# A skipping first turn of TensorE's loop, fold 6 behind values 7, and aligned starts with hinted ends on the other engines

## The chip, the cores and the metric

The kernel runs on one core of a Trainium2 chip. Time is device microseconds (us) of that core. Three runs of the kernel before gave a median of 185.13 us (184.97 to 185.88). The profiled execution took 185.13 us; from its first to its last instruction the profile counts a span of 183.2 us, and the other 1.93 us lie around it.

A core has five engines with an instruction stream each: TensorE (PE in the profile; PEld is its weight load), VectorE (DVE), ScalarE (ACT), GpSimd (POOL) and SyncE (SP). They wait for each other by semaphores. Loads and stores run on 16 DMA engines. Instructions come to an engine by DMA too; the profile lists those transfers as queues of kind "instruction".

## The reference

One decoding step of attention over a sliding window, with grouped heads: 32 sequences, 32 query heads, 8 key/value heads of 128 columns, and the last 512 of 2048 cached positions.

```python
W = min(4096, max(256, Sk // 4))                      # 512
q = (x @ wq).reshape(B, Sq, Hq, Dh).transpose(0, 2, 1, 3)
k = repeat(k_cache[:, :, Sk - W:, :], 4, axis=1)
v = repeat(v_cache[:, :, Sk - W:, :], 4, axis=1)
scores = einsum("bhqd,bhkd->bhqk", q, k) * (Dh ** -0.5)
o = einsum("bhqk,bhkd->bhqd", softmax(scores), v)
out = o.transpose(0, 2, 1, 3).reshape(B, Sq, Hq * Dh) @ wo
```

All inputs are bfloat16: `x` is 32x1x512, the caches are 32x8x2048x128, `wq` is 512x4096 and `wo` 4096x512. The windows of keys and values are 33.5 MB each, `wq` and `wo` 4.2 MB each: 75.5 MB have to be read.

## The kernel before, in words

The 32 sequences are worked in eight groups of four (q = 0 to 7, called quarters below, as each fills the 128 partitions with four sequences). For each of them 4 MB of keys and 4 MB of values are loaded, with one partition per sequence, head and block of 128 positions (32 KB in a row). There are two key buffers (`K_sb`) and two value buffers (`V_sb`); `wq` first lies in the second value buffer, and `wo` at the end in the first key buffer.

SyncE issues all loads but `x`, in the order of `LOADS` (L34): after `wq`, keys 0 and 1, values 0, keys 2 and 3, values 1, and from there keys and values in turn, each as soon as its buffer is free. Keys q wait for VectorE's second turn of keys q-2, values q for TensorE's values q-2. Values 5 to 7 come in halves, and `wo` in three pieces (`WOP`, L40, rows 0 to 16, 16 to 28 and 28 to 32), which wait for the keys of quarter 6 to be turned. `x` is issued by ScalarE (L199 to L202), ahead of everything else on that engine.

The work on a quarter has these steps; the letters are those of the order strings at the top of the file, a digit is the quarter:

- T: VectorE transposes the keys in two halves (L511, 4.4 us each).
- S: TensorE's scores, two halves of 16 matmuls (L340). GpSimd spreads the queries for them (L309).
- M, X, N: VectorE's row maximum, ScalarE's exponential with its sum, VectorE's division.
- E: TensorE brings the probabilities to the rows of the values (L356), and ScalarE copies them out (G, L574).
- B: VectorE and ScalarE each spread four heads of them into a block diagonal (L530, L578).
- P: TensorE's values, 128 matmuls over 32 groups (L367), in parts such as `P0.0.16`.
- C: VectorE or ScalarE copy the four row blocks out of PSUM (L536, L584). The last quarter is copied in halves, I (L541, L589).
- F: TensorE's fold, four float32 matmuls with a 0/1 matrix (L379), and D: ScalarE's copy of it into `o_sel` (L592).

TensorE runs a head (`PE_HEAD`, L20: scores of quarters 0 and 1, E0 and E1), then a loop (L430) of four turns with two rounds each, written by `PE_ROUND` (L21), then a tail (`PE_TAIL`: fold 7) and the output projection (L449), 128 small matmuls with four column groups side by side. Inside the loop the groups of S and E are skipped in the last turn by a branch (L443), as there are no quarters 8 and 9. Values of semaphores to wait for are computed from the loop's counter into registers (`looped`, L433). VectorE and ScalarE run their lists `DVE_OPS` and `ACT_OPS` (L24, L29) without a loop, and end with two copies each of the output; SyncE then stores it. The fold writes to a PSUM bank given by `f_bank` (L182): bank 2 of the half of PSUM that the quarter's values use, and bank 2 for fold 7.

The scores, sums, folds and copies are put in order by hand in these strings; a helper (`needs`, L105) turns them into waits. `Waits` (L218) leaves out waits that an engine has already made.

Of the kernel before, what the change touches and what calls it, by code (L numbers as in the profile page):

```python
# [21 lines left out]
PE_TAIL = "F7"  # L22
# [8 lines left out]
G5 C3.0.4 B5.4.8 D3 X6 G6 C4.0.4 B6.4.8 D4 X7 G7 C5.0.2 B7.4.8 D5 C6.0.2 D6 I7.0.0 I7.1.0 I7.0.1 I7.1.1 D7  # L31
# [15 lines left out]
def bass_standalone__sliding_block_cached__sampling_kernel(  # L47
# [25 lines left out]
    real = lambda w: w[0] not in "SE" or int(w[1:].split(".")[0]) < NQ  # L73
# [54 lines left out]
    with ExitStack() as es:  # L128
# [53 lines left out]
        def f_bank(q):  # L182
            return ps[:, 2] if q == NQ - 1 else ps[:, 4 * (q % 2) + 2]
# [14 lines left out]

        for b0, b1 in X_PARTS:  # L199
            nc.scalar.dma_start(  # L200
                x_sb[b0:b1, :], x[b0:b1].rearrange("b s d -> b (s d)")
            ).then_inc(sem_x, 16)  # L202
# [11 lines left out]
        def rows(cache, q, r0=0, r1=R):  # L214
            return cache[4 * q:4 * q + 4, :, SK - W:, :].rearrange(
                "b h (k r) d -> (b h) k (r d)", k=KB)[:, :, r0 * DH:r1 * DH]

# [98 lines left out]
        def _(pe):  # L316
# [132 lines left out]
            for j, (i0, i1) in enumerate(WOP):  # L449
                pe.wait_ge(sem_wo[j], 16)  # L450

                last = i1 == NI
                for cs in ((0, 1), (2, 3)) if last else ((0, 1, 2, 3),):
                    for i in range(i0, i1):
                        for c in cs:
                            ins = pe.matmul(  # L456
                                Y_ps[32 * c:32 * (c + 1), 0:P],
                                lhsT=o_sel[:, i, :],
                                rhs=wo_sb[:, i, c * P:(c + 1) * P],
                                start=i == 0, stop=i == NI - 1, tile_position=(0, 32 * c),  # L460
                            )
                    if last:
                        ins.then_inc(s["pe_Y"], 1)
# [14 lines left out]
        def _(dve):  # L478
# [70 lines left out]
            for c in (0, 2):  # L549
                dve.wait_ge(s["pe_Y"], c // 2 + 1)  # L550
                dve.tensor_copy(
                    out_sb[:, c, :], Y_ps[32 * c:32 * (c + 1), 0:P]
                ).then_inc(s["dve_y"], 1)

        @block.scalar
        def _(act):
# [41 lines left out]
            for op in orders["ACT"]:  # L598
                wait(needs(op))
                key, n = counter("ACT", op)  # L600
                run[op[0]](*op[1:]).then_inc(op_sem[key], n)
            for c in (1, 3):
                act.wait_ge(s["pe_Y"], c // 2 + 1)
                act.activation(
                    out_sb[:, c, :], Y_ps[32 * c:32 * (c + 1), 0:P], ACTF.Copy
                ).then_inc(s["act_y"], 1)
# [28 lines left out]
```

## Time and profile before

| | |
|---|---|
| median of 3 runs | 185.13 us |
| profiled execution | 185.13 us |
| its span | 183.2 us |
| read from memory | 75.53 MB, 412 GB/s over the span |
| TensorE matmuls busy | 122.3 us, 67% |
| VectorE busy | 102.6 us, 56% |
| ScalarE busy | 53.1 us, 29% |
| GpSimd busy | 17.5 us, 10% |
| mean granted TensorE clock | 0.823 |

The first part of a profile's page gives busy times per engine. The second part cuts the span in 40 slices of 4.58 us: a digit is the busy share of an engine in tenths, and the row "DMA" the mean share over 16 DMA engines. The third part lists the DMA queues: how many packets they had, how many MB, and what share of 16 engines' time these took. The trace behind the page can be asked for the same in any stretch; there, packets "under 512 B" are mostly the writes with which each of the 16 engines reports that its part of a load is there. The chain of waits is the work that ended last, followed back from the end; each piece has its start, its duration and its engine and line. Timelines give start, duration, engine, line and tiles, with the idle time ahead and what ended it.

### The profile page before, as it was taken

Reading aid. Unit: us, or ns where it says so; the run is one execution under the profiler, and the core shown is the slowest. Engines: PE = TensorE matmul, PEld = TensorE weight load, DVE = VectorE, ACT = ScalarE, POOL = GpSimd, SP = SyncE. Lnnn points to the kernel's source line nnn. Section 1 sums busy time; section 2 is a strip of 40 time slices with the busy share of each in tenths; the row PEclk is TensorE's granted clock in tenths of the full one; section 3 lists DMA queues with packets and bytes.
Section 4 is the critical chain, followed back from the end, with each engine's and each line's share of the span. In section 5 each row is a group of like instructions: output and inputs, shape, how many; then the busy total and the mean of one; then the engine's idle time right before and its main releaser. Section 6 shows DMA issues by size and latency. Waiting matters only on the chain.

```text
span 183.2 us, 3760 instructions
## 1 busy us (share of the span) xinstructions
PE 122.3 (67%) x1644; PEld 55.9 (30%) x1644; DVE 102.6 (56%) x103; ACT 53.1 (29%) x100; POOL 17.5 (10%) x55
## 2 busy tenths in 40 slices
PE   0089404445403997699389935992399499999964
PEld 0023101002300353255034502450144235454533
DVE  0030899996439718947970796079604992323031
ACT  3000400010391004802910391039102741462031
POOL 7900040101100010002000200020000000000000
PEclk9999955555855599699957985999569969999999
DMA  6998999899998999899999999999999999999980
GB/s 219 418 494 372 451 458 458 379 422 458 447 429 379 458 454 443 379 433 458 422 422 408 458 431 429 408 451 443 436 408 411 426 433 426 433 426 433 423 358 28
DMA packets 3576, 75.67 MB, mean 413 GB/s; under 512 B 432, under 2 KB 496, under 8 KB 624
## 3 DMA queue, kind: packets, MB, share of 16 engines
q1 hardware_dynamic: 3504, 75.53, 96.5%
q8 instruction: 5, 0.08, 0.2%
q10 hardware_dynamic: 64, 0.03, 0.1%
q14 instruction: 3, 0.02, 0.0%
HBM read 75.53 MB, written 0.03 MB: 412 GB/s over the span
## 4 chain that ended last, share of the span: by engine, by line
PE 44%; DMA 39%; DVE 12%; ACT 1%; issue 1%; ACTq 1%; DVEq 0%
PE ps L371 28%; DMA V_sb<-in_v_cache_dram 25%; DMA K_sb<-in_k_cache_dram 11%; DVE KT_sb L513 7%; PE ps L333 5%; PE ps L346 4%; PE ps L383 4%; DMA bd<-in_x_dram 4%; PE ps L359 2%; DVE QT_sb L505 2%; DVE KT_sb L502 1%; ACT C_sb L586 1%; PE ps L456 1%; DVE C_sb L542 1%; ACTq L200 1%
## 5 line engine op out<-in xcount | busy, mean ns | idle before, releaser
L371 PE MATMUL ps<-V_sb,bd 32*128 32x512 bf16 x1024 | 68.9, 421 | 7.4 <-DMA V_sb<-in_v_cache_dram 7.3
L513 DVE STREAM_TRANSPOSE KT_sb<-K_sb 128x4096 f32<-128x4096 f32 x16 | 70.1, 4421 | 3.4 <-DMA K_sb<-in_k_cache_dram 3.3
L346 PE MATMUL ps<-KT_sb,QBD 128*32 128x512 bf16 x256 | 23.3, 496 | 37.6 <-DVE KT_sb L513 25.1
L371 PEld LDWEIGHTS ps<-V_sb,bd 32*128 32x128 bf16 x1024 | 27.1, 102 | 47.3 <-issue 21.7
L519 DVE TENSOR_REDUCE maxv<-ps 128x1 f32<-128x512 f32 x8 | 5.5, 687 | 32.2 <-PE ps L346 32.2
L346 PEld LDWEIGHTS ps<-KT_sb,QBD 128*32 128x32 bf16 x256 | 6.2, 108 | 50.0 <-issue 21.8
L581 ACT ACTIVATE bd<-PTc,mask 128x512 bf16<-128x512 bf16 x32 | 20.3, 710 | 0.2
L309 POOL COPY QBD<-QT_sb 32x128 bf16<-32x128 bf16 x32 | 9.3, 289 | 101.8 <-PE ps L346 84.7
L568 ACT ACTIVATE P_f<-ps,negmax 128x512 f32<-128x512 f32 x8 | 5.5, 687 | 38.9 <-DVE negmax L521 38.9
L586 ACT ACTIVATE C_sb<-ps 32x512 f32<-32x512 f32 x24 | 14.1, 588 | 5.9 <-PE ps L371 5.7
L593 ACT ACTIVATE o_sel<-ps 128x128 bf16<-128x128 f32 x8 | 2.2, 278 | 39.0 <-PE ps L383 39.0
L383 PE MATMUL ps<-C_sb,F_sb 128*128 128x128 f32 x72 | 10.7, 289 | 1.2 <-DVE C_sb L542 1.2
L575 ACT ACTIVATE PTc<-ps 128x512 bf16<-128x512 f32 x8 | 4.8, 597 | 21.1 <-PE ps L359 21.1
L359 PE MATMUL ps<-P_bf,E_sb 128*128 128x128 bf16 x128 | 9.4, 231 | 2.1 <-DVE P_bf L527 2.1
L333 PE MATMUL ps<-V_sb,bd 128*128 128x512 bf16 x32 | 10.0, 490 | 0.8 <-DVE bd L481 0.8
L383 PEld LDWEIGHTS ps<-C_sb,F_sb 128*128 128x128 f32 x72 | 8.8, 191 | 5.3 <-issue 3.4
L359 PEld LDWEIGHTS ps<-P_bf,E_sb 128*128 128x128 bf16 x128 | 7.9, 104 | 5.7 <-DVE P_bf L527 4.9
L533 DVE TENSOR_SCALAR bd<-PTc,mask 128x512 bf16<-128x512 bf16 x32 | 8.9, 342 | 0.0
L538 DVE COPY C_sb<-ps 32x512 f32<-32x512 f32 x4 | 2.8, 693 | 8.1 <-PE ps L371 8.1
L502 DVE CAST KT_sb<-ps 128x512 bf16<-128x512 f32 x4 | 2.5, 683 | 7.5 <-PE ps L333 7.5
L321 PE MATMUL ps<-bd 32*128 32x128 bf16 x4 | 0.6, 295 | 8.9 <-DMA bd<-in_x_dram 8.9
L562 ACT ACTIVATE KT_sb<-ps 128x512 bf16<-128x512 f32 x4 | 2.1, 602 | 15.1 <-PE ps L333 15.1
(34 smaller groups left out, 36.3 us busy)
## 6 DMA issues: line engine op xcount, KB each, us to landing
K_sb<-in_k_cache_dram SPq DMA_DIRECT2D x8, 4096.0 KB, 22.2
V_sb<-in_v_cache_dram SPq DMA_DIRECT2D x5, 4096.0 KB, 25.5
V_sb<-in_v_cache_dram SPq DMA_DIRECT2D x6, 2048.0 KB, 17.5
V_sb<-in_wq_dram SPq DMA_DIRECT2D x2, 2048.0 KB, 9.7
K_sb<-in_wo_dram SPq DMA_DIRECT2D x1, 2048.0 KB, 15.4
K_sb<-in_wo_dram SPq DMA_DIRECT2D x1, 1536.0 KB, 18.5
K_sb<-in_wo_dram SPq DMA_DIRECT2D x1, 512.0 KB, 19.2
out_dram<-P_bf SPq DMA_DIRECT2D x1, 32.0 KB, 1.6
```

Source lines behind the costliest of these rows:

```text
L309: pool.tensor_copy(QBD[pr, q % 2].rearrange("p (w t) (h c) -> p w t h c", w=2, h=HKV)[:, :, :, :, 4 * b:4 * b + 4], QT_sb[pr, q].rearrange ...
L333: ins = pe.matmul(ps[:, n], lhsT=xT_sb[:, kt, :], rhs=wq_sb[:, kt, n * 512:(n + 1) * 512], start=kt == 0, stop=kt == DKT - 1, tile_positio ...
L346: ins = pe.matmul(s_bank(q)[32 * c:32 * c + 32, :], lhsT=QBD[:, q % 2, 2 * w + t, c0:c0 + 32], rhs=KT_sb[:, w, :, KB * h:KB * h + KB, t], ...
L359: ins = pe.matmul(e_bank(q)[:, e * R:(e + 1) * R], lhsT=E_sb[:, k, e].rearrange("p m j -> p (m j)"), rhs=P_bf[:, k * R:(k + 1) * R], start ...
L371: ins = pe.matmul(o_banks(q)[:, b, :], lhsT=bd[pr, q % 2, 4 * g:4 * g + 4].rearrange("p r h e -> p (r h e)"), rhs=V_sb[q % 2][pr, 512 * g: ...
L383: ins = pe.matmul(f_bank(q)[:, 0:P], lhsT=F_sb[:, d].rearrange("p h d -> p (h d)"), rhs=C_sb[:, q % 2, :, 32 * d:32 * d + 32], start=d == ...
L513: return dve.transpose(KT_sb[:, w].bitcast(F32).rearrange("p r c t -> p r (c t)"), K_sb[q % 2][:, :].bitcast(F32).rearrange("p (r w c) -> ...
L519: dve.tensor_reduce(maxv[:, q:q + 1], s_bank(q), AX.X, ALU.max).then_inc(s["dve_m"], 1)
L533: ins = dve.tensor_scalar(o, i, m, None, op0=ALU.mult)
L568: return act.activation(P_f32[:, :].rearrange("p (k r) -> p k r", k=KB), s_bank(q).rearrange("p (r k) -> p k r", k=KB), ACTF.Exp, bias=neg ...
L581: ins = act.activation(o, i, ACTF.Copy, scale=m)
L586: ins = act.activation(*pick_args(q, r), ACTF.Copy)
```

## The change

Four things are changed.

- TensorE's loop runs one turn more, ahead of the others, in which all groups are skipped: the counter goes from 0 to 8 by 2 instead of 0 to 6, and each half of a round stands in a branch that is left out for 0. The waits' values are computed from the new counter.
- Fold 6 is taken out of the last round, where it stood inside values 7, and put into the tail behind them, ahead of fold 7. In the last turn the second round's fold is skipped with its second half of scores. Fold 7 takes PSUM bank 1, as fold 6 now uses bank 2 at the same time. On ScalarE the copy of fold 6 (D6) moves behind the four half copies of values 7.
- VectorE, ScalarE and GpSimd get an alignment ahead of their first instruction: what follows begins at a multiple of 128 instructions, and an engine jumps over the padding.
- A loop of exactly one turn (`single`) is put around TensorE's output projection, and around the last part of VectorE's list (from M7 on) and of ScalarE's (from X7 on). Its only use is its closing branch, which is announced as likely taken by a hint at the top of the loop, and which is not taken.

```diff
-PE_TAIL = "F7"
+PE_TAIL = "F6 F7"
...
-G5 ... C6.0.2 D6 I7.0.0 I7.1.0 I7.0.1 I7.1.1 D7
+G5 ... C6.0.2 I7.0.0 I7.1.0 I7.0.1 I7.1.1 D6 D7
...
-    real = lambda w: w[0] not in "SE" or int(w[1:].split(".")[0]) < NQ
+    real = lambda w: int(w[1:].split(".")[0]) < NQ and w != f"F{NQ - 2}"
...
-            return ps[:, 2] if q == NQ - 1 else ps[:, 4 * (q % 2) + 2]
+            return ps[:, 1] if q == NQ - 1 else ps[:, 4 * (q % 2) + 2]
...
+        for engine in (nc.scalar, nc.vector, nc.gpsimd):
+            engine.addr_align(128, offset=0, max_nops=0)
         for b0, b1 in X_PARTS:
             nc.scalar.dma_start(
...
+        def single(eng):
+
+            once = eng.alloc_register("once")
+            eng.reg_mov(once, 1)
+            return nc.Fori(0, once, 1, engines=[eng.engine], hint_back_edge=True)
...
-            with nc.Fori(0, ROUNDS, 2, engines=[mybir.EngineType.PE]) as i:
+            with nc.Fori(0, ROUNDS + 2, 2, engines=[mybir.EngineType.PE]) as turn:
                 held = {}
 
                 def looped(q, a, b):
                     key = (skipped, a, a * q + b)
                     if key not in held:
-                        v = i * a + (a * q + b)
-                        held[key] = pe.snap(v & 7 if key == (False, 1, 3) else v)
+                        least = a * (q - 2) + b
+                        v = turn * a + least
+                        mask = 7 if key == (False, 1, 3) else 127 if least < 1 else 0
+                        held[key] = pe.snap(v & mask if mask else v)
                     return held[key]
 
                 for p in range(2):
                     words = PE_ROUND.format(p - 1, p, p + 1, p + 2).split()
-                    for skipped, group in groupby(words, lambda w: w[0] in "SE"):
-                        with pe.If(i < NQ - 2) if skipped else nullcontext():
-                            for op in ops_of(" ".join(group)):
-                                do(op, looped)
+                    for part in (words[:4], words[4:]):
+                        with pe.If(turn >= 2):
+                            for skipped, group in groupby(part, lambda w: w[0] in "SE" or p == 1 and w[0] == "F"):
+                                with pe.If(turn < NQ) if skipped else nullcontext():
+                                    for op in ops_of(" ".join(group)):
+                                        do(op, looped)
...
-            for j, (i0, i1) in enumerate(WOP):
-                pe.wait_ge(sem_wo[j], 16)
+            with single(pe):
+                for j, (i0, i1) in enumerate(WOP):
+                    pe.wait_ge(sem_wo[j], 16)
...
-            for op in orders["DVE"]:
-                wait(needs(op))
-                key, n = counter("DVE", op)
-                run[op[0]](*op[1:]).then_inc(op_sem[key], n)
...
+            cut = orders["DVE"].index(("M", NQ - 1))
+            do(orders["DVE"][:cut])
+            with single(dve):
+                do(orders["DVE"][cut:])
+                for c in (0, 2):
+                    dve.wait_ge(s["pe_Y"], c // 2 + 1)
...
+            cut = orders["ACT"].index(("X", NQ - 1))
+            do(orders["ACT"][:cut])
+            with single(act):
+                do(orders["ACT"][cut:])
```

More of the change, by code (lines that the diff above doesn't have):

```diff
@@ L30 @@
 X0 G0 X1 G1 B0.4.8 B1.4.8 X2 G2 C0.0.4 B2.4.8 D0 X3 G3 C1.0.4 B3.4.8 D1 X4 G4 C2.0.4 B4.4.8 D2 X5
-G5 C3.0.4 B5.4.8 D3 X6 G6 C4.0.4 B6.4.8 D4 X7 G7 C5.0.2 B7.4.8 D5 C6.0.2 D6 I7.0.0 I7.1.0 I7.0.1 I7.1.1 D7
+G5 C3.0.4 B5.4.8 D3 X6 G6 C4.0.4 B6.4.8 D4 X7 G7 C5.0.2 B7.4.8 D5 C6.0.2 I7.0.0 I7.1.0 I7.0.1 I7.1.1 D6 D7
 """
@@ L448, in _ @@
             wait([ends["D", NQ - 1]])
-            for j, (i0, i1) in enumerate(WOP):
-                pe.wait_ge(sem_wo[j], 16)
[L452 to L463, printed above, removed]
+            with single(pe):
+                for j, (i0, i1) in enumerate(WOP):
+                    pe.wait_ge(sem_wo[j], 16)
+                    last = i1 == NI
+                    for cs in ((0, 1), (2, 3)) if last else ((0, 1, 2, 3),):
+                        for i in range(i0, i1):
+                            for c in cs:
+                                ins = pe.matmul(
+                                    Y_ps[32 * c:32 * (c + 1), 0:P],
+                                    lhsT=o_sel[:, i, :],
+                                    rhs=wo_sb[:, i, c * P:(c + 1) * P],
+                                    start=i == 0, stop=i == NI - 1, tile_position=(0, 32 * c),
+                                )
+                        if last:
+                            ins.then_inc(s["pe_Y"], 1)
         def spread_args(q, h):
@@ L544, in _, with do @@
             run = {"T": turn, "M": maxes, "N": norm, "B": spread, "C": pick, "I": pick_half}
-            for op in orders["DVE"]:
-                wait(needs(op))
-                key, n = counter("DVE", op)
-                run[op[0]](*op[1:]).then_inc(op_sem[key], n)
[L549 to L553, printed above, removed]
+            def do(ops):
+                for op in ops:
+                    wait(needs(op))
+                    key, n = counter("DVE", op)
+                    run[op[0]](*op[1:]).then_inc(op_sem[key], n)
+            cut = orders["DVE"].index(("M", NQ - 1))
[4 more added lines that the diff above has]
+                    dve.wait_ge(s["pe_Y"], c // 2 + 1)
+                    dve.tensor_copy(
+                        out_sb[:, c, :], Y_ps[32 * c:32 * (c + 1), 0:P]
+                    ).then_inc(s["dve_y"], 1)
         @block.scalar
@@ L597, in _, with do @@
             run = {"X": exponential, "G": gather, "B": spread, "C": pick, "I": pick_half, "D": folded}
[L598 to L606, printed above, removed]
+            def do(ops):
+                for op in ops:
+                    wait(needs(op))
+                    key, n = counter("ACT", op)
+                    run[op[0]](*op[1:]).then_inc(op_sem[key], n)
+            cut = orders["ACT"].index(("X", NQ - 1))
+            do(orders["ACT"][:cut])
+            with single(act):
+                do(orders["ACT"][cut:])
+                for c in (1, 3):
+                    act.wait_ge(s["pe_Y"], c // 2 + 1)
+                    act.activation(
+                        out_sb[:, c, :], Y_ps[32 * c:32 * (c + 1), 0:P], ACTF.Copy
+                    ).then_inc(s["act_y"], 1)
 _INS = ['x', 'k_cache', 'v_cache', 'wq', 'wo']
```

## The prediction

> **What bounds the kernel now.** I read the page's slices and queues first, since a share of 96.5% names a suspect:
>
> ```profile
> DMA  6998999899998999899999999999999999999980
> q1 hardware_dynamic: 3504, 75.53, 96.5%
> q8 instruction: 5, 0.08, 0.2%
> q14 instruction: 3, 0.02, 0.0%
> ```
>
> The 16 DMA engines are busy from slice 1 to slice 38, so the loads set the pace. 75.53 MB in 183.2 us is 412 GB/s; an undisturbed stretch of the trace (107 to 180) runs at about 430. Instructions are loaded by DMA too: five packets for TensorE on q8 (0.08 MB, so 16 KB each) and three of 8 KB on q14. Their bytes are nothing, but each is one packet on one engine, and a load is complete only when all 16 engines have written their completion (the packets under 512 B). So I asked the trace's DMA view for short windows around the end of a load. Four answers, windows 41.4 to 41.9, 47.7 to 49, 51.1 to 51.6 and 52.7 to 53.1:
>
> ```profile
> DMA packets 30, 0.49 MB, mean 983 GB/s; under 512 B 15, under 2 KB 15, under 8 KB 15
> q8 instruction: 1, 0.02, 5.2%
> DMA packets 28, 0.46 MB, mean 918 GB/s; under 512 B 14, under 2 KB 14, under 8 KB 14
> DMA packets 2, 0.03 MB, mean 82 GB/s; under 512 B 1, under 2 KB 1, under 8 KB 1
> ```
>
> Values 0 completes within half a microsecond. Then TensorE's first fetch comes (5.2% of 16 engines over 1.3 us is 1.08 us on one). Of the next load, keys 2, fourteen of the 16 completions come together (one stands just ahead of the window) and the last comes alone 1.5 us later, with none between. At 70.5 to 71.1 fourteen are there and two come at 72.2 to 72.6, after the second fetch (68 to 70); three are late after the third (80 to 82), and a fourth fetch follows in 87.5 to 89.5. So every 16 KB fetch sets one engine back by about 1.5 us, each time another engine, and nothing lets it catch up, for the stream never pauses. Queued work is ample: values 2 are issued at 72.30, when keys 4 (whose first engines end at about 80.5) are still running. The small fetches take 0.3 to 0.44 us, between 87.5 and 106.5.
>
> Last, the end of the chain of waits and the last load's row:
>
> ```profile
> 175.61 0.02 issue
> 175.64 0.42 DVE C_sb L542
> ...
> 177.49 0.72 PE ps L383 x4
> 178.22 0.02 issue
> 178.24 0.29 ACT o_sel L593
> 178.53 0.04 issue
> 178.57 1.98 PE ps L456 x128
> 180.55 0.02 issue
> 180.58 0.28 DVE P_bf L551
> ```
> ```profile
> DMA to landing us min/median/max: 15.4/18.5/19.2
> ```
>
> The three pieces of the output weight are issued at 159.7, 160.3 and 160.8 and so land at 175.1, 178.8 and 180.0 (the last one's semaphore is full at 180.06). The output matmuls (128, 15.5 ns each) run through from 178.57; those on the last piece begin 112 x 15.5 ns = 1.73 us in, at 180.30. The compute chain is thus only 0.24 us behind the last load. Both limits stand side by side at the end, and a gain on one is capped by the other.
>
> **The change part by part.** The sum is made against the profiled execution: 185.13 us, 183.2 of span and 1.93 around it; it is also the median of the runs.
>
> *Fold 6 behind values 7.* Now fold 6 stands inside the last values (170.86, 1.09 us to the next matmul). Moved behind them it lets values 7 end at 175.64 - 1.09 = 174.55; their second half is in by then, since 2 MB (4.9 us) of output weight landing at 175.1 follow it in the queue: 170.2, against a start at 170.87. Fold 6 runs 174.55 to 175.64 while VectorE and ScalarE copy values 7 in halves (1.80 us on DVE, to 176.36). Fold 7's first half could start at 175.43 and is held 0.2 us; its second half waits for the copies anyway, so nothing is lost. Fold 7 ends near 177.13, ScalarE's `o_sel` copy near 177.45 (that of fold 6, 0.28 us, moves into the gap at 176.14), and the output matmuls start at 177.50 instead of 178.57. Compute gains 1.07 us. Of that only the part up to the last load counts: with the load at 180.06 as now, 0.04 us to start and 16 x 15.5 ns = 0.25, they end at 180.35 instead of 180.55. Gain: 0.20 us.
>
> *The turn that skips all.* TensorE ends its head at 50.12 and then stands idle until 57.97, for the first turned keys of quarter 2:
>
> ```profile
> 49.05 1.07 PE L359 MATMUL ps<-P_bf,E_sb 128*128 128x128 bf16 x16 [2.08 <-DVE P_bf L527]
> 57.97 0.62 PE L346 MATMUL ps<-KT_sb,QBD 128*32 128x512 bf16 x4 [7.86 <-DVE KT_sb L513]
> ```
>
> The built program (two instructions to a matmul) has 275 slots ahead of the loop and 773 in it, so with 256 slots to 16 KB the loop lies in four blocks. The skipping turn jumps through them and asks for the three not yet fetched, at about 50 to 57 instead of 68, 80 and 88. No row of before has TensorE waiting on a block. Bounds: nothing at best; at worst each of the two or three jumps into a missing block waits for a whole fetch, some 1.3 us to begin (the fourth packet lies that far behind the entry into its block) and 1.05 to run, 7 us in all. 7.85 us are free, so I take nothing. Should it be double, 14 us, the first values end 6.3 us late and values 2 are issued at 78.6, still before 80.5: no pause in the stream. Keys (VectorE's turns behind scores 2, SP's key loads) have as much in hand, 8 us and more at each issue.
>
> [...]
>
> *More branches and registers.* Per turn four tests (`turn >= 2`), one more skipped group and some ten register steps, on TensorE's sequencer. Today's step over the back edge, with a test and registers, costs 0.09 us (159.10 to 159.19). Ten such in the last turn would be 0.9 us, nothing at best; the 0.83 us by which compute would be ahead of the last load (180.06 - 177.50 - 1.73) covers all but this end. I take nothing, as ahead of a full queue they are hidden.
>
> *The fetch block and the hinted ends.* VectorE (132 slots), ScalarE (about 120) and GpSimd (about 70) jump once to a boundary of 128 slots. Their next block (8 KB) is then fetched at the start and not at 88, 91 and 106. If the boundary's block is absent, ScalarE's x loads wait for it: 2.4 us by the fetch above, nothing if it is there. TensorE's first matmul (8.89) and all behind it would slip as much; SP isn't aligned, its first five loads need no one, and the sixth, keys 2, is issued 7 us before values 0 run out (33.78 against 41). GpSimd's and VectorE's first work has that cover as well. Three set-backs of 0.3 to 0.6 us (1.46/1.05 of their packets) leave the middle of the stream, on engines that were not the last. That gains nothing, and it costs something only if one now shares an engine with a 16 KB fetch. The hint may spare the fifth TensorE packet; that one ran 180.5 to 181.8 beside nothing that was awaited. The single-turn loops add a jump and a register step in front of waits: nothing.
>
> Sum: 185.13 - 0.20 = 184.9 us. The first fetch, at 47.7, comes ahead of the loop, where no TensorE instruction is changed; so one engine still ends 1.5 us late.
>
> **The rivals.**
> *Slower: two large fetches on one DMA engine.* The skipping turn jumps into blocks whose fetch is under way, and may ask for them again, or the close succession may put two on one engine. That engine would be 2 x 1.46 behind; the last load lands at 181.5 and all behind it follows: 184.9 + 1.46 = 186.4. [...] Against: four fetches took four engines, and back edges asked for nothing. It decides as soon as one engine has served two q8 packets ahead of the last load.
> *Faster: the set-backs vanish.* If early fetches cost the last load nothing, it lands at about 178.6, and compute is the limit with its full 1.07: 184.06. For it: the change moves three of four fetches into one stretch and the small ones to the start. Against: the first stays, and one is enough. A shorter 1.93 around the span, if the engines' ends load less, would come to the same; no row shows it.
> *Neither: a small fetch at the start on the engine of a large one.* 0.3 to 0.6 us onto the last load: 185.2 to 185.5.
>
> **How the numbers follow.** Forecast 184.9: 0.55. Small collision: 0.08. Vanished set-backs: 0.20. Doubled: 0.17. About 0.5% (0.93 us) is what a measurement of this kernel can tell from no change: faster 0.20, within 0.63, slower 0.17. The range leaves out the doubled case: from 184.06, less the 0.16 that the fastest run lies below the median, 183.9, to 185.5 and half of the slowest run's 0.75 more, 185.9. The likeliest alone: 184.6 to 185.2.
>
> **What would show it.** The output matmuls starting near 177.5 and pausing for the last piece, which lands near 180.0; q8 packets at 47.7 and three more before 60, none from 60 to 175; q14 packets near 1 to 3 us; keys 4 late on more engines than before, each by no more than 1.5 us. Wrong if the last piece lands before 179 or after 181, or if the first scores in the loop start well after 58 and an issue to DMA comes too late.

## The result: about 1% slower, and the profile after

The changed kernel took 187.01 us (median of four runs, 186.38 to 188.15) beside 185.28 us for the kernel before on the same chip: 1.0106 of its time, interval 1.0078 to 1.0133. The forecast was 184.9 us and the range ended at 185.9; none of the four runs lies inside. Four more runs of it later (e5 below) had a median of 188.0 us, 1.0144 [1.0112, 1.0177]. Ratios leave out slow executions, more than 1.5% above the fastest of their kernel (one of e2 and two of e9, the profiled one among these); medians and ranges hold them.

The profiled execution took 186.38 us, the fastest of the first four: 184.3 us of span and 2.08 around it. First the page's slices and queues:

```profile
DMA  6998999989999999999999999999999999999970
q1 hardware_dynamic: 3504, 75.53, 96.1%
q8 instruction: 4, 0.07, 0.1%
q14 instruction: 5, 0.03, 0.1%
```

The same 75.53 MB move on engines that look as busy as before. TensorE has four instruction packets instead of five, the other engines five small ones instead of three. What these shares hide is in the chain of waits (start, duration, what), here its start and its middle:

```profile
1.16 2.44 ACTq L202
...
4.42 6.64 DMA bd<-in_x_dram
...
57.84 7.03 issue
64.87 1.90 PE ps L354 x16
```

The first two of these rows before:

```profile
0.74 0.55 ACTq L200
...
1.97 6.79 DMA bd<-in_x_dram
```

ScalarE's first DMA issue takes 2.44 us (0.55 before), so `x` is there at 11.06 instead of 8.76. And the first scores of the loop begin at 64.87 instead of 57.97. Before, they waited for VectorE's keys; now the keys are ready at 57.84, and TensorE starts 7.03 us later, in a stretch in which it waits for nothing that the profile shows ("issue"). The queue views of four short windows (48.5 to 50.5, 54 to 56.5, 60.5 to 62.5, 67 to 68.6) tell what happens there:

```profile
q8 instruction: 1, 0.02, 3.4%
q8 instruction: 1, 0.02, 2.7%
q8 instruction: 1, 0.02, 3.2%
q8 instruction: 1, 0.02, 4.0%
```

Each holds one instruction packet of TensorE. Their starts are 48.95, 54.91, 61.14 and 67.36, 6.0 to 6.2 us apart, though each packet takes only about 1.05 us. TensorE's head ends at 51.87 and the skipping turn takes it through blocks that arrive one by one: of the branches of L453, 0.07 us in the median, one takes 5.58 us from 51.79 and the next 6.24 us from 57.43. Its 13.00 us up to the first scores are 3.04 to the packet at 54.91, 6.23 to the one at 61.14, 1.03 while that one runs, and 2.7 more; the packet at 67.36 comes behind the first scores. So two packets were waited for, not three. SyncE's issue of values 2 before and after (timelines of SP):

```profile
72.30 0.53 SPq L248 DMA_DIRECT2D V_sb<-in_v_cache_dram  x1
```
```profile
78.93 0.53 SPq L256 DMA_DIRECT2D V_sb<-in_v_cache_dram  x1
```

The end of the span, from the timeline (start, duration, engine, line, operation, and in brackets the idle time ahead with what ended it):

```profile
177.36 1.08 PE L469 MATMUL ps<-K_sb,o_sel 128*32 128x128 bf16 x64 [0.65 <-ACT o_sel L612]
179.05 0.85 PE L469 MATMUL ps<-K_sb,o_sel 128*32 128x128 bf16 x48 [0.61 <-DMA K_sb<-in_wo_dram]
180.27 0.43 PE L469 MATMUL ps<-K_sb,o_sel 128*32 128x128 bf16 x16 [0.36 <-DMA K_sb<-in_wo_dram]
```

The output matmuls start at 177.36 instead of 178.57 and pause for the last two pieces of `wo`. The last piece lands at 180.22 (180.06 before). The final copies begin at 180.71, 0.13 us later than before. The rest of the loss is behind them, in the queue view from 181.5 on:

```profile
DMA  0000000000964200000000000000000000000000
GB/s 0 0 0 0 0 0 0 0 0 0 234 161 103 59 0 0 0 0 0 29 0 0 0 0 0 0 0 0 0 0 0 0 0 0 0 0 0 0 0 0
q14 instruction: 1, 0.01, 1.4%
out_dram<-P_bf SPq DMA_DIRECT2D x1, 32.0 KB, 2.5
```

An 8 KB instruction packet runs at 182.2, just as the output is stored. Of the store's pieces the last two come alone (the 29 of the second row) some 0.4 us behind the others, and the store takes 2.5 us from issue to landing. The same row before:

```profile
out_dram<-P_bf SPq DMA_DIRECT2D x1, 32.0 KB, 1.6
```

So this execution's 1.25 us are 0.13 up to the copies, 0.9 in the store and about 0.2 outside the span. That is the fastest execution, however. The others were 0.6 to 1.8 us slower still, and the profile of e5 (188.41 us) shows another loss beside the one in the store.

### The profile page after: what moved, and what is told of

Same layout as the page of the kernel before. It is cut to its first block, busy times and chain, and to the rows that moved or that the text cites. A ratio compares the mean times of both kernels' runs of the same rounds, so it can differ in the third digit from the quotient of the medians.

```text
span 184.3 us, 3844 instructions
## 1 busy us (share of the span) xinstructions
PE 114.9 (62%) x1644; PEld 54.9 (30%) x1644; DVE 102.7 (56%) x103; ACT 53.0 (29%) x100; POOL 17.4 (9%) x55
## 3 DMA queue, kind: packets, MB, share of 16 engines
q1 hardware_dynamic: 3504, 75.53, 96.1%
HBM read 75.53 MB, written 0.03 MB: 410 GB/s over the span
## 4 chain that ended last, share of the span: by engine, by line
DMA 39%; PE 37%; DVE 11%; issue 5%; ACT 4%; ACTq 2%; SPq 1%; DVEq 0%
PE ps L379 22%; DMA V_sb<-in_v_cache_dram 13%; DMA K_sb<-in_wo_dram 11%; DMA K_sb<-in_k_cache_dram 10%; DVE KT_sb L526 7%; PE ps L354 5%; PE ps L341 4%; ACT C_sb L605 4%; DMA bd<-in_x_dram 4%; PE ps L391 3%; PE ps L367 3%; DVE QT_sb L518 2%; ACTq L202 2%; DVE KT_sb L515 1%; SPq L262 1%
## 5 line engine op out<-in xcount | busy, mean ns | idle before, releaser
L379 PE MATMUL ps<-V_sb,bd 32*128 32x512 bf16 x1024 | 64.1, 399 | 7.1 <-DMA V_sb<-in_v_cache_dram 6.6
L354 PE MATMUL ps<-KT_sb,QBD 128*32 128x512 bf16 x256 | 21.0, 456 | 42.9 <-DVE KT_sb L526 17.3
L379 PEld LDWEIGHTS ps<-V_sb,bd 32*128 32x128 bf16 x1024 | 25.9, 98 | 42.4 <-issue 12.2
L367 PE MATMUL ps<-P_bf,E_sb 128*128 128x128 bf16 x128 | 10.2, 243 | 2.1 <-DVE P_bf L540 2.1
L367 PEld LDWEIGHTS ps<-P_bf,E_sb 128*128 128x128 bf16 x128 | 8.6, 110 | 5.7 <-DVE P_bf L540 4.9
L341 PE MATMUL ps<-V_sb,bd 128*128 128x512 bf16 x32 | 8.7, 438 | 0.8 <-DVE bd L494 0.8
L494 DVE CAST bd<-ps 128x512 bf16<-128x512 f32 x1 | 0.7, 690 | 11.8 <-PE ps L329 11.8
```

Of the source, the lines that this page charges most:

```text
L341: ins = pe.matmul(ps[:, n], lhsT=xT_sb[:, kt, :], rhs=wq_sb[:, kt, n * 512:(n + 1) * 512], start=kt == 0, stop=kt == DKT - 1, tile_positio ...
L354: ins = pe.matmul(s_bank(q)[32 * c:32 * c + 32, :], lhsT=QBD[:, q % 2, 2 * w + t, c0:c0 + 32], rhs=KT_sb[:, w, :, KB * h:KB * h + KB, t], ...
L367: ins = pe.matmul(e_bank(q)[:, e * R:(e + 1) * R], lhsT=E_sb[:, k, e].rearrange("p m j -> p (m j)"), rhs=P_bf[:, k * R:(k + 1) * R], start ...
L379: ins = pe.matmul(o_banks(q)[:, b, :], lhsT=bd[pr, q % 2, 4 * g:4 * g + 4].rearrange("p r h e -> p (r h e)"), rhs=V_sb[q % 2][pr, 512 * g: ...
```

## The experiments

The theories are numbered in the expectations as they came up. 1: an instruction fetch of VectorE, moved by its alignment, runs beside the output store. 2: the skipping turn alone, by making TensorE late. 3: the later `x` and the fetches at the start alone. 4: the later `x` and the skipping turn together make values 2 so late that the DMA queues run dry near 80 us. Ratios are to the kernel before, run on the same chip beside each.

### One part out, or one part alone: e1 to e4

e1, on the changed kernel: VectorE's single-turn loop taken out.

```diff
-            with single(dve):
+            with nullcontext():
```

> The changed kernel, but VectorE's last part stands in no single-turn loop (its alignment stays). That takes six instructions from VectorE and moves the boundary of 128 slots behind its last copies and its barrier. Theory 1 (the loss is at the end: VectorE steps over a boundary at its closing branch, and the 8 KB fetch that follows holds one DMA engine of the output store): the store lands in 1.6 us again instead of 2.5, all 16 completions within 0.3 us, span near 183.4, time 0.9 us below the changed kernel, about 186.1 (185.5 for an execution like the profiled one). Theory 2 (the skipping turn costs it, by the late values 2 and the pause in the stream at 80 us): no change against the changed kernel, 186.4 to 187.0. Theory 3 (the later x load and the fetches at the start cost it): no change either.

Measured: 187.09 us (185.89 to 188.55), 1.0138 [1.0083, 1.0194]. The fetch was still there, at 182.13, and the store took 2.2 us. Six instructions fewer did not take the fetch away from the store, so this neither supports nor refutes theory 1; its expectation failed. The loop on VectorE is not the cause of the loss.

e2, on the changed kernel: no alignment, and no single-turn loops on VectorE and ScalarE; TensorE's parts stay.

```diff
-        for engine in (nc.scalar, nc.vector, nc.gpsimd):
-            engine.addr_align(128, offset=0, max_nops=0)
...
-            with single(dve):
+            with nullcontext():
...
-            with single(act):
+            with nullcontext():
```

> Only TensorE's parts of the change: the skipping turn, fold 6 behind values 7 and the hinted loop round the output projection. No alignment and no single-turn loop on the other engines. Theory 1 (fetch at the end beside the store): 184.9 to 185.3, the store in 1.6 us. Theory 2 (skipping turn): 186.2 or more, the last piece of the output weight landing later than 180.5. Theory 3 (start): 184.9 to 185.3, with x landing near 8.6 as before.

Measured: 185.27 us (184.69 to 187.79), 1.0014 [0.9995, 1.0034]. The loss is gone from the median, with the skipping turn still in. Half of the ten executions lie between 184.7 and 185.1; one is at 187.79, without a profile. The profiled one (185.83 us) has a store delayed by another fetch, one of TensorE's at 181.14; queue view from 181 on:

```profile
q8 instruction: 1, 0.02, 3.1%
out_dram<-P_bf SPq DMA_DIRECT2D x1, 32.0 KB, 2.6
```

e3, on the kernel before: the skipping turn alone (the loop's part of the diff, with fold 6 where it was).

```diff
-            with nc.Fori(0, ROUNDS, 2, engines=[mybir.EngineType.PE]) as i:
+            with nc.Fori(0, ROUNDS + 2, 2, engines=[mybir.EngineType.PE]) as turn:
...
-                    for skipped, group in groupby(words, lambda w: w[0] in "SE"):
-                        with pe.If(i < NQ - 2) if skipped else nullcontext():
-                            for op in ops_of(" ".join(group)):
-                                do(op, looped)
+                    for part in (words[:4], words[4:]):
+                        with pe.If(turn >= 2):
+                            for skipped, group in groupby(part, lambda w: w[0] in "SE"):
+                                with pe.If(turn < NQ) if skipped else nullcontext():
+                                    for op in ops_of(" ".join(group)):
+                                        do(op, looped)
```

> The kernel before with the skipping turn alone. TensorE's first scores in the loop should start near 65 instead of 58, with fetches near 48, 54, 60 and 66, in any theory. Theory 1 and theory 3: 185.0 to 185.4, as the last load still lands near 180.1 and the engines that were ahead lose what the pause at 80 us takes. Theory 2: 186.2 or more.

Measured: 185.67 us (184.7 to 186.42), 1.0019 [0.9993, 1.0046]. The first scores of the loop come at 63.42 and values 2 are issued at 77.05, 4.75 us later than before, and the time hardly moves. The median lies between what the theories gave (up to 185.4, or 186.2 and more); the profile decides: the last piece of `wo` lands at 180.12, as before (180.06). Theory 2 falls: for the loads, the lateness of the skipping turn alone is covered. Not so for the compute chain, which still has fold 6 inside the values: the output matmuls start 0.83 us later than before (178.57) and the copies at 181.40 instead of 180.58.

```profile
179.40 1.98 PE L467 MATMUL ps<-K_sb,o_sel 128*32 128x128 bf16 x128 [0.37 <-ACT o_sel L610]
```

e4, on the changed kernel: the skipping turn taken out, all the rest in.

```diff
-            with nc.Fori(0, ROUNDS + 2, 2, engines=[mybir.EngineType.PE]) as turn:
+            with nc.Fori(0, ROUNDS, 2, engines=[mybir.EngineType.PE]) as i:
...
-                    for part in (words[:4], words[4:]):
-                        with pe.If(turn >= 2):
```

> The changed kernel without the skipping turn (the loop of the kernel before): fold, alignment and single-turn loops are in. Theory 1: the store still lands in 2.5 us and the time is 186.0 to 186.8. Theory 2: 184.9 to 185.3. Theory 3: 186.0 to 186.8 with the loss ahead of the last load, which would land near 181.

Measured: 185.83 us (185.52 to 187.02), 1.0038 [1.0022, 1.0054]. `x` is late here (first matmul at 11.93), but the first scores of the loop come at 57.90, as before: the late `x` alone is covered as well, and theory 3 falls. What stays is the store, 2.2 us with the fetch at 181.89; all runs but one lie 0.6 to 1.1 us above the 184.9 of before. So removing the skipping turn takes away the larger share of the loss and leaves a smaller one.

### The dry queue: e5, e7, e10, e11

e5 is the changed kernel again.

> The changed kernel once more, for a second profile and to have it on the chip of the next three. Theory 1 (a fetch beside the output store): the profile again shows an 8 KB fetch after 181 and one completion of the store late by 0.5 to 1.2 us. Theory 4 (the two together: with x late by 2 us AND the skipping turn, values 2 are issued so late that the stream runs dry near 80 us, by more in some executions than in others): an execution at 187 or more shows values 2 issued after 79.5 and a pause of 1 us or more in the loads near 80; one at 186.4 or less shows none beyond 0.6.

Measured: 188.0 us (187.4 to 188.47), 1.0144 [1.0112, 1.0177]. The profiled execution, SyncE's timeline:

```profile
82.13 0.54 SPq L256 DMA_DIRECT2D V_sb<-in_v_cache_dram  x1
```

and the stretches around it (start and end, length, busy shares of PE, PEld, DVE, ACT and POOL with their instructions, the granted TensorE clock, the DMA share, GB/s):

```profile
80.00:81.00 1.00, 1.00 (x20) 0.90 (x16) 1.00 (x1) 0.00 (x0) 0.00 (x0) 1.00 0.31 131
81.00:82.00 1.00, 1.00 (x18) 0.32 (x16) 1.00 (x1) 0.60 (x1) 0.00 (x0) 1.00 0.08 33
82.00:83.00 1.00, 0.08 (x4) 0.00 (x0) 1.00 (x1) 0.85 (x2) 0.00 (x0) 1.00 0.00 0
83.00:84.00 1.00, 0.00 (x0) 0.00 (x0) 1.00 (x1) 0.98 (x3) 0.00 (x0) 1.00 1.82 492
```

Values 2 are issued at 82.13. The first engines had run empty at 80.4 and the last at 82.3, and the next packets of a load start at 83.45. They come 1.3 us behind the issue (1.31 to 1.33 in e5, e7, e9, e10, e11 and e16). The last piece of `wo` lands at 182.48 instead of 180.06. The store is delayed here too, as theory 1 had it: an 8 KB packet at 184.46, and 2.3 us from issue to landing. In the first profile of the changed kernel values 2 were issued at 78.93, the moved bytes dipped only to 197 GB/s between 81 and 82, and values 2 landed 9.71 us behind keys 4, as before (9.80). So the same program stands on both sides of an edge.

e7, on the changed kernel: no single-turn loop on ScalarE.

```diff
-            with single(act):
+            with nullcontext():
```

> The changed kernel without ScalarE's single-turn loop (aligned as there): six instructions fewer on ScalarE. Theory 1 with ScalarE as the one that steps over a boundary: the fetch after 181 comes later than the store (after 183) or not at all, and the best execution falls by 0.9 us to 185.5. Theory 4: executions at 187 and more still occur, as x is late and the skipping turn is in. If the fetch stays at 182, it is not ScalarE's loop that makes the step.

Measured: 186.84 us (185.66 to 187.92), 1.0089 [1.0056, 1.0122]. The loop isn't the cause of the dry queue. In its profile values 2 were issued at 79.20, and two engines brought them 2 us later than the rest (landing 11.35 behind keys 4). The 8 KB fetch came at 184.06, 1.17 us behind the store's issue instead of 0.84, and just missed the store, which took 1.5 us; the time lies where it was all the same. So late values 2 alone make such a time.

e10, on e2: ScalarE's alignment put back, nothing else.

```diff
+        for engine in (nc.scalar,):
+            engine.addr_align(128, offset=0, max_nops=0)
```

> TensorE's parts (skipping turn, fold 6 behind values 7, hinted loop) and ScalarE's alignment alone; VectorE and GpSimd as before, no loop on VectorE and ScalarE. Theory 4 (late x and skipping turn together): x lands near 10.5, TensorE's first scores in the loop at 64 to 68, values 2 issued at 78 to 82, executions spread from 185.3 to 188; where they are issued after 79.5 the profile has a pause in the loads near 80. Theory 2 (skipping turn alone) and theory 1: like the run with TensorE's parts alone, 184.7 to 185.8.

Measured: 188.31 us (186.66 to 188.74), 1.0163 [1.0098, 1.0228], against 1.0014 without that alignment. The profiled execution (187.9 us): the issue, the first scores of the loop and one window.

```profile
81.39 0.53 SPq L256 DMA_DIRECT2D V_sb<-in_v_cache_dram  x1
```
```profile
67.17 1.90 PE L354 MATMUL ps<-KT_sb,QBD 128*32 128x512 bf16 x16 [14.16 <-issue]
```
```profile
81.00:82.00 1.00, 0.35 (x8) 0.00 (x0) 1.00 (x1) 0.60 (x3) 0.00 (x0) 1.00 0.00 0
```

The head of TensorE ends at 53.01 (49.96 in e3), then it stands 14.16 us ("issue"; as I read it, for its blocks), and values 2 are issued when the queues are already empty. The store took 1.5 us. This is theory 4 with one alignment switched.

e11, on the kernel before: two skipping turns instead of none, one run.

```diff
-            with nc.Fori(0, ROUNDS, 2, engines=[mybir.EngineType.PE]) as i:
+            with nc.Fori(0, ROUNDS + 4, 2, engines=[mybir.EngineType.PE]) as turn:
...
+                        with pe.If(turn >= 4):
```

> The kernel before with two skipping turns ahead of the loop's work. If the first skipping turn is slow because of blocks that are not there (three jumps at 6 us), the second costs under 1 us: first scores in the loop at 63.5 to 64.5, and no more than four 16 KB fetches by then. If jumps and branches themselves are slow, or each turn fetches anew, the scores start at 69 or later and the stream runs dry near 80.

Measured: 188.0 us, one execution, so without an interval. The first scores come at 64.97, 1.55 us later than with one skipping turn (63.42); I had expected less than 1. TensorE's large packets are four by 65.6, as with one: the second skipping turn fetched nothing anew. Values 2 are issued at 79.03 and land 11.69 us behind keys 4, on one engine that is 2 us late. Not all of the 188.0 us is the queue's: the last piece of `wo` lands 1.85 us later than before (181.91), but the copies begin 3.08 us later (183.66), as the compute chain with fold 6 in its old place is late too (e3).

### The lateness by itself: e13, e14, e16

To take the fetches and the alignment out of the question, these put idle matmuls of 128x512 ahead of the loop of the kernel before (with fold 6 moved): 48, 72 and 96.

```diff
+            for _ in range(96):
+                pe.matmul(
+                    Y_ps, lhsT=E_sb[:, 0, 0].rearrange("p m j -> p (m j)"),
+                    rhs=E_sb[:, 0].rearrange("p e m j -> p (e m j)"),
+                    start=True, stop=True, tile_position=(0, 0),
+                )
```

> The kernel before with the fold moved, and 48 matmuls of 128x512 into a free PSUM bank between TensorE's head and its loop, whose result nobody reads: extra work, the output is the reference's. No skipping turn, no alignment. At 0.43 us each for some 14 and then 0.21 us they last about 13 us, so the first scores start near 63.5 and values 2 are issued near 76.5. If it is the lateness of values 2 that costs and 79 is where it begins: 184.9 to 185.1, no pause. If any lateness of TensorE costs in proportion (5.5 us here): 186 or more.

> The same with 72 such matmuls: about 18 us, first scores near 68.5, values 2 issued near 81.7. If the lateness of values 2 is the cause of the loss: a pause in the loads from 80.4 to 83 and 187 to 187.6 (landing of values 2 about 11.8 us behind keys 4 instead of 9.7), without any jump into a missing block. If it is the fetches that the skipping turn asks for, or the late x: 184.9 to 185.2.

> As the kernels with 48 and 72 extra matmuls, now with 96 (24 x 0.213 = 5.1 us more than 72): first scores near 71.4, values 2 issued near 82.7, beyond the point. If the lateness of values 2 is the cause: the loads pause from 80.4 to about 84, values 2 land 11.8 to 12.2 us behind keys 4 and all 16 engines close together again, time 187.0 to 188.0. If it is the skipping turn's fetches or the late x that cost, and not lateness: 184.9 to 185.4.

Measured:

| | first scores | values 2 issued | landing behind keys 4 | last piece of `wo` | time | ratio |
|---|---|---|---|---|---|---|
| e13, 48 | 62.37 | 73.77 | 9.72 | 180.03 | 184.91 | 0.9975 [0.9957, 0.9992] |
| e14, 72 | 66.25 | 77.65 | 9.70 | 180.40 | 185.38 | 0.9998 [0.9974, 1.0023] |
| e16, 96 | 71.43 | 82.83 | 13.77 | 184.32 | 189.45 | 1.0234 [1.0198, 1.0269] |

The 48 and 72 matmuls made less delay than I had reckoned (values 2 at 73.77 and 77.65 instead of 76.5 and 81.7; the mean granted clock was 0.860 and 0.884, 0.823 before; the 0.43 us a matmul, reckoned for 14 as at L333 in before, lasted only to 54.1 and 52.3, and then 0.21), so e14 ended on the near side of the edge and e16 had to follow. e16 lost more than expected (189.45 us instead of 187.0 to 188.0): fifteen engines report values 2 by 94.96, the last at 96.14, and a 16 KB packet of TensorE at 91.08 would fit that; it is not shown. Its windows:

```profile
81.00:82.00 1.00, 1.00 (x23) 0.78 (x24) 1.00 (x1) 0.15 (x1) 0.00 (x0) 1.00 0.00 0
82.00:83.00 1.00, 0.78 (x16) 0.17 (x8) 1.00 (x1) 0.61 (x2) 0.00 (x0) 1.00 0.00 0
83.00:84.00 1.00, 0.00 (x0) 0.00 (x0) 1.00 (x1) 0.99 (x2) 0.00 (x0) 1.00 0.00 0
84.00:85.00 1.00, 0.00 (x0) 0.00 (x0) 1.00 (x2) 0.98 (x3) 0.00 (x0) 1.00 1.90 524
```

No skipping turn, no alignment, no hint, and the same pause with a store of 1.5 us. Lateness of values 2 alone is enough for the pause and the loss.

### The late x and the store apart: e6, e9, e12, e15

e6, on the changed kernel: ScalarE not aligned.

```diff
-        for engine in (nc.scalar, nc.vector, nc.gpsimd):
+        for engine in (nc.vector, nc.gpsimd):
```

> The changed kernel with VectorE and GpSimd aligned, but not ScalarE (its single-turn loop stays). x should land near 8.6 again instead of 10.6, and TensorE's first scores in the loop a microsecond earlier (64). Theory 1: if the fetch after 181 is ScalarE's, it goes or moves, and the store takes 1.6 us: 185.2 to 185.6 in all. Theory 4: no pause near 80, so the executions near 188 go; 185.0 to 186.0. If neither holds, it stays at 186.4 to 187.1.

Measured: 186.1 us (185.77 to 186.27), 1.0054 [1.0038, 1.0071]. The issues of `x` (timeline of ScalarE) begin at 0.73, the first matmul is at 9.45 (11.20 in the changed kernel), and values 2 are issued at 76.69. No pause any more, and no executions at 187 or above, though the median is just above the 185.0 to 186.0 of theory 4. All seven are 0.8 to 1.3 us above before, and the queue view of the end shows why (the fetch, at 182.22, has stayed, so it is not ScalarE's):

```profile
q14 instruction: 1, 0.01, 0.9%
out_dram<-P_bf SPq DMA_DIRECT2D x1, 32.0 KB, 2.2
```

e9, on the changed kernel: VectorE aligned to slot 16 of its block instead of 0, so that its next boundary comes earlier in its list.

```diff
-            engine.addr_align(128, offset=0, max_nops=0)
+            engine.addr_align(128, offset=16 if engine is nc.vector else 0, max_nops=0)
```

> The changed kernel with VectorE's alignment at slot 16 of a block of 128 instead of slot 0; nothing else. Its boundary then falls at its 112th instruction, near the last maximum (155 us), and not at the end. Theory 1 with VectorE as the one that steps over: the fetch that came 0.9 us behind the last copies is gone, one of 8 KB stands near 150 to 156, and the store lands 1.5 to 1.7 us after its issue with all 16 completions within 0.4 us; best execution 185.5. If the fetch beside the store stays, it is not VectorE's. Theory 4: executions at 187 and more go on, each with values 2 issued after 79.

Measured: 186.86 us (185.25 to 189.19), 1.0087 [1.0054, 1.0119]. The queue view of 150 to 152, and the one of the end:

```profile
q14 instruction: 1, 0.01, 1.0%
```
```profile
out_dram<-P_bf SPq DMA_DIRECT2D x1, 32.0 KB, 1.5
```

The packet has moved to 151.15 and the store is as short as before: the fetch beside the store is VectorE's, set there by its alignment. e15 below has it at 149.71, with a store of 1.5 us. This profile has the other loss instead (values 2 at 82.19, a pause from 80.4 to 83.5). I read the wide scatter as executions on both sides of the edge.

e12, on the kernel before: fold 6 moved, and VectorE's alignment and loop, nothing else.

```diff
-PE_TAIL = "F7"
+PE_TAIL = "F6 F7"
...
+        for engine in (nc.vector,):
+            engine.addr_align(128, offset=0, max_nops=0)
...
+            with single(dve):
+                do(orders["DVE"][cut:])
```

> The kernel before with fold 6 behind values 7 and VectorE's alignment and single-turn loop alone. Theory 1 with VectorE: an 8 KB fetch 0.9 us behind its last copies (near 182), one completion of the store late by 0.4 to 1.2 us, 185.5 in all against 184.95 for the fold alone. Not VectorE: no fetch there, 184.9.

Measured: 184.90 us (184.73 to 185.06), 0.9988 [0.9971, 1.0005]. A miss: I had expected 185.5. The fetch is there, at 182.275, but lasts 0.36 us and the store takes 1.6. So a fetch near the store doesn't always delay it. The traces show what decides. In every profile the store's pieces start from 0.86 us behind its issue on. The 8 KB fetch starts 0.81 to 0.84 us behind the issue in e1, e4, e5, e6 and the first profile of the changed kernel, and the store takes 2.16 to 2.5 us; in e7 and e12 it starts 1.17 us behind, and the store takes 1.5 and 1.6. In these seven profiles the fetch is early wherever ScalarE's single-turn loop is in and late where it is out (e7, e12); why is open.

e15, on the changed kernel: ScalarE not aligned, VectorE at slot 16.

```diff
-        for engine in (nc.scalar, nc.vector, nc.gpsimd):
-            engine.addr_align(128, offset=0, max_nops=0)
+        nc.vector.addr_align(128, offset=16, max_nops=0)
+        nc.gpsimd.addr_align(128, offset=0, max_nops=0)
```

> The changed kernel, ScalarE not aligned and VectorE aligned to slot 16 instead of 0; skipping turn, fold, GpSimd's alignment and all single-turn loops stay. x lands near 8.6, values 2 are issued at 76 to 78.5, the 8 KB fetch of VectorE stands near 151: no pause and no fetch beside the store. If those two things are the whole loss: 184.8 to 185.2, as the kernel before. If something else in the change costs, 185.5 or more.

Measured: 185.34 us (184.99 to 187.47), 1.0013 [0.9979, 1.0047]. The median is just above the 184.8 to 185.2 expected and below 185.5. With both causes out, the skipping turn, the hints and GpSimd's alignment cost nothing that this can measure. Values 2 are issued at 78.06 in the profile (185.38 us), and two of ten executions still lie at 186.3 and 187.5: near the edge, as I read it, though neither of the two was profiled.

### Fold 6 alone: e8, e17

On the kernel before, fold 6 moved behind values 7 and D6 behind the half copies, twice the same kernel.

```diff
-PE_TAIL = "F7"
+PE_TAIL = "F6 F7"
...
-                    for skipped, group in groupby(words, lambda w: w[0] in "SE"):
+                    for skipped, group in groupby(words, lambda w: w[0] in "SE" or p == 1 and w[0] == "F"):
```

> The kernel before with fold 6 behind values 7 alone (with its bank and its copy's place). All theories: output matmuls start near 177.5 and end 0.1 to 0.2 us earlier, against the last load; 0.1 to 0.2 us below the kernel before, ratio 0.999.

> The kernel before with the fold moved alone, once more, since in the earlier run its times were closer together than those of the kernel before (184.7 to 185.35 against 184.8 to 185.8). If that holds: median 184.9 to 185.0, none above 185.4, ratio 0.997 to 0.9995. If not: the same spread as the kernel before.

Measured: 184.97 us (184.71 to 185.35), 0.9992 [0.9979, 1.0005], and 184.94 us (184.79 to 185.04), 0.9981 [0.9965, 0.9997]. It is the version that beats both kernels: by 0.2% in the second set, and by as much in e13, which has it too (0.9975), while the first set can't be told from no gain. In the profiles the copies begin at 180.62 (e8), against 180.58 before, so a single execution shows no gain at the end. What differs is that the kernel before has a group of executions at 185.6 to 186.0 that neither set of fold 6 has, nor e12 and e13 (184.73 to 185.13). A cause that would fit is TensorE's last instruction packet. In the kernel before it ends at 181.76, close to the store's pieces from 182.09 on, and in these two at 181.35 and 181.41, some 0.75 us ahead of the pieces; in e2, where it ran until 182.56, it covered them and the store took 2.6 us. For the kernel before that is argued, not shown.

### What they say together

The issue of values 2 and what followed, over all profiles (time of the profiled execution in the last column):

| values 2 issued | kernels | landing behind keys 4 | us |
|---|---|---|---|
| 70.4 to 73.8 | before, e4, e8, e12, e13, e17 | 9.71 to 9.80 | 184.9 to 185.1 (e4: 187.0, of it 3.4 outside the span) |
| 76.4 to 78.93 | e1, e2, e3, e6, e14, e15, changed | 9.70 to 9.95 | 185.3 to 186.4 |
| 79.03, 79.20 | e11, e7 | 11.69, 11.35 | 188.0, 186.8 |
| 81.4 to 82.2 | e5, e9, e10 | 11.60 to 12.14 | 187.9 to 188.4 |
| 82.83 | e16 | 13.77 | 189.2 |

Theory 4 holds: both delays are on the chain that leads to values 2, each alone stays below 79 us (72.16 in e4; 76.4 to 78.1 in e2, e3, e6, e15) and both together end at 78.6 to 82.2. Theory 1 holds too: the fetch is VectorE's (e9, e15), and where it runs as the store's pieces start (e1, e4, e5, e6 and the first profile) the store takes 0.55 to 0.9 us more than the 1.6 of before; e7 and e12 had the fetch 0.3 us later and no delay. The profile of e5 has both losses: of its 3.28 us, 2.4 lie ahead of the copies and 0.7 in the store.

## Why the prediction was wrong, and where it was right

**The set-backs by instruction fetches** were read rightly. The last load was bound as before, at 180.22 (foretold near 180.0), the small fetches came mostly at the start (1.77, 1.80, 3.80), and the added turn fetched no block twice: four packets for five turns. The 256 slots to 16 KB, on which the four blocks rest, are borne out by the trace of before: between its first and its fourth packet (47.73 and 87.82) TensorE has 384 matmuls and 384 weight loads, 768 slots to three packets, and only some 30 branches, waits and register steps besides. The rival by which two large fetches fall on one engine is not what happened: the engines complete keys 4 within 2.06 us (80.22 to 82.28), where two fetches would have set one back by 2 x 1.46 = 2.9.

**Fold 6** was right in its mechanism and in the place: start at 177.36 (foretold 177.50), pause for the last piece, cap by the load. The term was mis-sized: the 16 last matmuls take 0.43 us after a pause and not 16 x 15.5 ns = 0.25, which leaves nothing of the 0.20 us in one execution; the load itself landed 0.16 us later than before.

**The turn that skips all** is the first step that failed. I priced a jump at 1.3 + 1.05 us, from fetches that lay ahead of sequential work; a jump into a missing block took 5.58 and 6.24 at its branch, and there were two of them. The bound "double, 14 us" was nearly the measured value: with the skipping turn and an early `x` (e2, e3, e6, e15) TensorE stood 13 to 14 us, and values 2 were issued at 76.4 to 78.1, against 78.6 foretold for that case. But I let that case pass by comparing 78.6 with 80.5, the moment when the first engines run empty. The packets come 1.3 us behind the issue and the first engines are empty at 80.3 to 80.4, so the point is near 79, and 78.6 had 0.4 us in hand, not 1.9. (14 us less the 7.85 that were free are 6.15, not 6.3, so the sum should have given 78.45.) The prediction's last sign of being wrong, first scores well after 58 and an issue that comes too late, is what came.

**The late x** was bounded at 2.4 us, which the first profile bears out (2.3 at `x`), but over the profiles the first matmul slips by 2.3 to 4.2 us (most in e9 and e10). It was wrongly waved through. I wrote that the first matmul and all behind it would slip as much and checked that slip against 7 us of cover, while the skipping turn had been given the same kind of cover. Both delays are on one chain. In the profiles with both, TensorE's head ends at 51.7 to 53.2 instead of 50.1, and 13 to 16 us of jumps follow. The sum of the two was never formed; e10 against e2 is the price of that, 1.0163 against 1.0014.

**The fetch block and the hinted ends.** I had VectorE's 132 slots and the block of 128 side by side and didn't conclude that the aligned list steps over its next boundary a few instructions before its end, at the store (its 8 KB packet at 182.20; with the start 16 slots on it stood at 151.15 in e9 and 149.71 in e15). I said of a fetch that it costs "only if one now shares an engine with a 16 KB fetch"; it also costs beside a short store that nothing covers: 0.9 us in the first profile.

**Branches and registers, single-turn loops** cost nothing measurable in the time, as forecast (e15, and e1 beside the changed kernel). The branches do take time: the step over the last back edge is 0.45 us in e3 and in the changed kernel (up to 157.95) instead of 0.09. In the changed kernel that is hidden, as TensorE waits 0.78 us for values 7 (at 170.47); in e3 it is 0.36 of the 0.83 us that the compute chain loses. ScalarE's loop goes with the early fetch at the store, as said under e12. The fifth TensorE packet is not in the record of the changed kernel, as supposed; in e2 it came at 181.14 and delayed the store, so "beside nothing that was awaited" holds only while it keeps clear of the store.

## What to carry to other kernels

Delays that are each covered have to be added up along the chain they share before they are held against the cover, and the cover of a DMA issue ends earlier than the queue does: here 1.3 us earlier. Where an engine's instruction list meets a block boundary is a place in the schedule like any other, so look what stands beside it, first of all a short store at the end: here that store took 2.5 us beside the fetch, and 1.5 with the fetch moved to 151.15. And the jump ahead to touch code early was paid with a stall at each block that had to be waited for (5.58 and 6.24 us in the changed kernel); the 13 to 14 us in all were covered only where nothing else was late.

## What the runs showed that I had not expected

- A jump of TensorE into a block that isn't loaded took 5.58 and 6.24 us at its branch in the changed kernel, while the DMA engines were full; the packets lie as far apart (48.95, 54.91, 61.14, 67.36; in e5 at 51.2, 57.7, 64.8, 70.9), though one packet takes only 1.05. Of the two branches, 3.1 and 3.7 us lie ahead of the packet and 1.4 and 1.5 behind it. What fills them the trace doesn't tell; a wait of the packet behind queued loads would fit the first, but wasn't tried.
- A pause need not cost what it lasts. The engines that had been set back by fetches go on while the others are idle: in e5 the spread between engines falls from 2.0 us (completions of keys 4) to 0.65 (values 2), and a pause of 3.1 us moves the last piece of `wo` by 2.4. In e9 and e10 the landing of values 2 is moved by less than the pause as well (2.5 of 3.1 and 1.7 of 2.3 us), but the last piece of `wo` by the whole of it (3.2 and 2.3); later instruction packets that set single engines back again would fit, but that is not shown.
- When the queues only just run dry (79.03 and 79.20), one or two engines bring values 2 about 2 us later than the others (e11, e7). Why is open.
- After its alignment ScalarE's first DMA issue takes 2.44 us instead of 0.55; without it, in e6, it is as quick as before. That this is a fetch of the boundary's block is likely by the packets at 1.77 and 1.80, and more so by e10, where ScalarE alone is aligned: one early packet, at 1.79, and a first issue of 2.89 us. In e6 the third issue took 1.45 us, beside a packet at 1.74. What an issue waits for no trace tells.
- Also open: why the fifth TensorE packet comes near 181 in e2, near 186 in e4 and not at all in the changed kernel; and why the profiled execution of e4 has 3.4 us outside its span, where its other runs have about 2.
